# Recurrent states kept by pairs of heads instead of by threes in a fused mLSTM and mixture-of-experts kernel

## The chip, the cores and the metric

The kernel runs on one core of one Trainium2 chip. The metric is the device time of one execution, in microseconds (us). The core has a matrix engine (TensorE, PE in the profile), whose weight loads are listed as an engine of their own (PEld), a vector engine (DVE), a scalar engine (ACT), a general engine (POOL) and a queue engine that issues DMAs (SP). PE multiplies a stationary operand, which has to be loaded first, by a moving operand, and writes the products into banks of PSUM; a float32 multiplication is run as two passes over the same operands, and the trace lists each pass as a load and a matmul. So a group of three float32 matmuls stands there as x6.

## What is computed

An mLSTM layer (2 batches, 8 heads, 768 steps, heads of 40), then a dense feed-forward layer with 2048 hidden units, then 8 experts whose outputs are weighted by a gate that is normalised by rows and columns. Only the first part bears on the change:

```python
for t in range(S):
    m_new = np.maximum(f_gate[:, :, t] + m, i_gate[:, :, t])
    f_stab = np.exp(f_gate[:, :, t] + m - m_new)
    i_stab = np.exp(i_gate[:, :, t] - m_new)
    C = f_stab[..., None, None] * C + i_stab[..., None, None] * np.einsum('bhd,bhe->bhde', vt, kt)
    n = f_stab[..., None] * n + i_stab[..., None] * kt
    h_tilde = np.einsum('bhde,bhe->bhd', C, qt)
    nq = np.einsum('bhd,bhd->bh', n, qt)[:, :, None]
    y[:, :, t] = o * h_tilde / np.maximum(np.abs(nq), 1.0)
x = y.reshape(1536, 320)
x = np.maximum(0.01 * (x @ w_in), x @ w_in) @ w_out          # then the experts, on x
```

## The kernel before

The sequence is cut into 6 pieces of 128 steps, which with 2 batches makes 12 chunks (`c0` to `c11`; even ones belong to batch 0, odd ones to batch 1). Within a chunk the recurrence is a masked product: scores of keys and queries (`sc`), weighted by decays (`ap`, `ex`, `wg`), times the values (`va`). What crosses from chunk to chunk is a state per head, 40 keys by 41 columns (40 values and the normaliser). Three steps of a chunk deal with it:

- `state` (`dp`, line 619): the weighted keys `kw` of three heads side by side, 120 columns, are the stationary operand, and the values of the three heads, 123 columns, the moving one. Of the 3 by 3 blocks of the product only the diagonal ones are wanted. Eight heads make G = 3 groups, with a ninth head of zeros. Chunks 0 to 9 do it.
- `carry` (`cr`, lines 660 to 665): the product `dps` is multiplied by a table `bdm` that is 1 on the diagonal blocks, and added to the state `Cst`, which is multiplied by its decay `decC` in the same instruction: one DVE instruction of 120x369 and three of 120x123. In chunks 0 and 1 it is one instruction that writes the masked product.
- `recall` (`zp`, line 613): the queries of three heads, stacked on 120 rows, are the stationary operand (128 columns, one for each step), and `Cst` of the group is the moving one (123 columns). Chunks 2 to 11 do it. These queries come in a load of their own, `q3`; the scores use another copy, `qP`, in which head pairs lie on rows 0 to 39 and 64 to 103.

The decays of the states are made twice (`nL` and `qL`, line 475): three matmuls with a table `ex` of 120 columns, loaded by DMA, spread a decay of each head over the head's rows, and an exponential on ACT writes `decC`.

The first 41 steps of the dense layer (`u`: up, `d`: down) and chunks 0 to 5 are laid out by the table `ORDER`: each engine runs its instructions in the order of that table. On PE it also holds matmuls on zeros that nothing reads (`w8@p` is eight of them), which stand where PE would be idle. SP issues the loads in the table's order as well. From chunk 6 on the program is written by a loop, and a scheduler orders it. After the dense layer come the experts, which the change doesn't touch. A step of the dense layer is 8 matmuls up (line 223) and 12 down (lines 230 to 232); the down matmuls stand three steps behind the up ones in the loop.

At the start PE waits for the gates: SP loads gates and the small table `rco`; DVE runs scans over the gates (lines 412 to 431); ACT splits numbers in halves (`a5` and `a6`, lines 437 and 438); DVE joins them (`a7`, line 441, writes `mv`) and spreads them (`c0.bd`, line 559), which the first decay matmul of chunk 0 reads (`c0.ap0`, line 566). The output of chunk 0 (`c0.ou`, DVE line 643) is turned by PE (`c0.tt`, line 335). DVE weighs the keys of some chunks (`kw`, line 602), POOL those of others (`c1`, `c2`, `c3`); the masking of decays (line 576) and some low halves of weights (`px`, line 215) are POOL's too.

## Time and profile before

| | before |
|---|---|
| median of 3 runs | 931.91 us (931.9 to 932.8) |
| the profiled execution | 931.88 us |
| its span, first to last instruction | 930.1 us |
| PE busy | 924.2 us, 99% |
| DVE / ACT / POOL busy | 587.3 / 490.1 / 552.1 us |
| DMA engines, mean share of the first 25 us | 0.85 |

The 1.8 us between the profiled time and its span lie before the first and after the last instruction. Busy time of PE counts overlapping passes once, so it tells that PE has work, not that the work is dense; the views that show waits and the distances between passes are needed beside it.

### The profile page before, as it was taken

How to read it: one execution, taken by the hardware profiler on the slowest of the kernel's cores; microseconds unless marked ns; L12 is line 12 of the kernel's file. 1: busy time of each engine (PE TensorE's matmuls, PEld its weight loads, DVE VectorE, ACT ScalarE, POOL GpSimd, SP SyncE). 2: the span in 40 equal slices, each digit the busy share in tenths (PEclk: the TensorE clock that was granted, in tenths of full speed). 3: DMA queues.
4: the chain of work that ended last, by engine and by line, in shares of the span. 5: the costliest groups of instructions: out<-in, count | busy, mean ns of one | idle time of the engine just before them, and what ended most of it. 6: DMA issues, size and time to landing. Idle time of an engine off the chain costs nothing.

```text
span 930.1 us, 16892 instructions
## 1 busy us (share of the span) xinstructions
PE 924.2 (99%) x6192; PEld 903.2 (97%) x6192; DVE 587.3 (63%) x1180; ACT 490.1 (53%) x959; POOL 552.1 (59%) x574
## 2 busy tenths in 40 slices
PE   9999999999999999999999999999999999999998
PEld 5899999999999999999999999999999999999998
DVE  8998751523958587666656665665666565666655
ACT  6877445345763645555445445544544455454442
POOL 3330244443442756767777777777777777767762
PEclk9999999999999999999999999999999999999999
DMA  8773131110301110111111111111111111111002
GB/s 273 253 233 129 34 111 31 56 39 3 88 14 33 52 38 24 52 38 38 37 38 53 46 52 38 37 38 38 50 48 50 41 38 38 38 49 49 30 2 85
DMA packets 57384, 56.49 MB, mean 61 GB/s; under 512 B 7654, under 2 KB 48086, under 8 KB 57302
## 3 DMA queue, kind: packets, MB, share of 16 engines
q1 hardware_dynamic: 57302, 55.43, 19.7%
q8 instruction: 48, 0.79, 0.4%
q14 instruction: 34, 0.28, 0.1%
HBM read 53.43 MB, written 1.97 MB: 60 GB/s over the span
## 4 chain that ended last, share of the span: by engine, by line
PE 94%; DVE 3%; ACT 1%; DMA 1%; issue 1%; SPq 0%; ACTq 0%; DVEq 0%
PE y L230 12%; PE y L231 12%; PE y L232 12%; PE ha L223 9%; PE b L1030 8%; PE b L1031 8%; PE b L1033 8%; PE b L1032 8%; PE ya L230 3%; PE ya L232 3%; PE ya L231 3%; PE yps L607 2%; PE sps L591 1%; PE zps L613 1%; PE dps L619 1%
## 5 line engine op out<-in xcount | busy, mean ns | idle before, releaser
L1054 POOL TENSOR_TENSOR hl<-c,hh 128x384 fp32r<-128x384 f32 x192 | 197.3, 1028 | 180.2 <-ACT c L1053 155.5
L230 PE MATMUL y<-w_e,hh 128*128 128x320 f32 x768 | 238.6, 311 | 0.0
L231 PE MATMUL y<-w_e,hh 128*128 128x320 f32 x768 | 237.0, 309 | 0.0
L232 PE MATMUL y<-w_e,hl 128*128 128x320 f32 x768 | 236.9, 308 | 0.0
L1112 DVE SCALAR_TENSOR_TENSOR acc<-y,Pg,acc 128x320 f32<-128x320 f32 x336 | 179.1, 548 | 63.4 <-PE y L232 56.3
L1052 ACT ACTIVATE hh<-c 128x384 fp32r<-128x384 f32 x192 | 99.8, 520 | 208.5 <-DVE c L1049 208.5
L1030 PE MATMUL b<-X,w_e 128*128 128x384 f32 x448 | 152.7, 341 | 0.2 <-DVE s L1070 0.2
L1031 PE MATMUL b<-X,w_e 128*128 128x384 f32 x448 | 151.0, 337 | 0.0
L1033 PE MATMUL b<-X,w_e 96*128 96x384 f32 x448 | 151.0, 337 | 0.0
L1032 PE MATMUL b<-X,w_e 128*128 128x384 f32 x448 | 150.9, 337 | 0.0
L230 PEld LDWEIGHTS y<-w_e,hh 128*128 128x128 f32 x768 | 144.3, 188 | 1.7 <-DVE acc L1110 1.1
L231 PEld LDWEIGHTS y<-w_e,hh 128*128 128x128 f32 x768 | 144.3, 188 | 0.0
L232 PEld LDWEIGHTS y<-w_e,hl 128*128 128x128 f32 x768 | 144.2, 188 | 0.0
L1053 ACT ACTIVATE c<-c 128x384 f32<-128x384 f32 x192 | 101.0, 526 | 18.0 <-ACT hh L1052 0.7
L1049 DVE TENSOR_TENSOR c<-b,s 128x384 f32<-128x384 f32 x192 | 100.6, 550 | 13.4 <-PE b L1033 10.0
L223 PE MATMUL ha<-xT,w_a 128*128 128x256 f32 x768 | 107.8, 285 | 0.0
L223 PEld LDWEIGHTS ha<-xT,w_a 128*128 128x128 f32 x768 | 100.1, 190 | 1.1 <-ACT gg L712 0.2
L1077 DVE SCALAR_TENSOR_TENSOR hl<-b,hh 128x384 fp32r<-128x384 f32 x64 | 35.6, 557 | 95.4 <-ACT hh L1076 95.4
L723 POOL TENSOR_TENSOR hla<-gg,hha 128x256 fp32r<-128x256 f32 x64 | 49.3, 772 | 70.3 <-ACT hha L718 62.4
L259 POOL TENSOR_TENSOR raw_e<-raw_e 128x256 f32<-128x256 f32 x116 | 85.2, 743 | 4.5
L1030 PEld LDWEIGHTS b<-X,w_e 128*128 128x128 f32 x448 | 84.8, 189 | 1.3 <-DVE s L1070 0.6
L1031 PEld LDWEIGHTS b<-X,w_e 128*128 128x128 f32 x448 | 85.3, 190 | 0.0
(200 smaller groups left out, 1496.7 us busy)
## 6 DMA issues: line engine op xcount, KB each, us to landing
raw_e<-in_w_dram SPq DMA_DIRECT2D x31, 320.0 KB, 2.9
raw_e<-in_w_dram SPq DMA_DIRECT2D x62, 128.0 KB, 2.2
raw_e<-in_w_dram SPq DMA_DIRECT2D x248, 32.0 KB, 1.9
raws<-in_w_in_dram SPq DMA_DIRECT2D x8, 768.0 KB, 5.9
rawU<-in_w_out_dram SPq DMA_DIRECT2D x4, 640.0 KB, 5.6
R<-in_kp_dram SPq DMA_DIRECT2D x10, 256.0 KB, 3.4
R<-in_qp_dram SPq DMA_DIRECT2D x10, 256.0 KB, 3.6
raws<-in_w_out_dram SPq DMA_DIRECT2D x4, 640.0 KB, 4.6
```

The lines of the kernel that those rows point to most:

```text
L223: nc.tensor.matmul(h_ps, t1[:, ws, c * P:(c + 1) * P], xt[:, xs, t0:t0 + n], start=(j == 0), stop=(j == len(MM1) - 1),)
L230: nc.tensor.matmul(y_ps, a, t2[:, c, :], start=first, stop=False)
L231: nc.tensor.matmul(y_ps, a, t2[:, 2 + c, :], start=False, stop=False)
L232: nc.tensor.matmul(y_ps, b, t2[:, c, :], start=False, stop=last)
L1030: nc.tensor.matmul(bank, f[:, 0], b[:, 0], start=fresh, stop=False, skip_group_check=not fresh)
L1031: nc.tensor.matmul(bank, f[:, 0], b[:, 2], start=False, stop=False, skip_group_check=not fresh)
L1032: nc.tensor.matmul(bank, f[:, 2], b[:, 0], start=False, stop=False, skip_group_check=not fresh)
L1033: nc.tensor.matmul(bank, f[0:K3, 1], b[0:K3, 1], start=False, stop=True, skip_group_check=not fresh)
L1049: nc.vector.tensor_tensor(c, part, plus, op=ALU.add)
L1053: nc.scalar.activation(c, c, AF.Relu)
L1054: nc.gpsimd.tensor_tensor(hl[a][b], c, hh[a][b].bitcast(F32), op=ALU.subtract)
L1112: nc.vector.scalar_tensor_tensor(out=o, in0=y, scalar=Pg[:, 2 * HP * q + t, e:e + 1], in1=o, op0=ALU.mult, op1=ALU.add)
```

## The change

Heads are kept in pairs: G = 4 groups of two heads, on rows 0 to 39 and 64 to 103, as `qP` already has them.

- `recall` reads `qP` (rows 0 to 103); the load `q3` and its place are gone. `qP` of odd and even chunks has a place each, since it is now read later.
- `state` has 4 matmuls with 104 stationary columns (the weighted keys lie 64 apart, with zeros between) and 82 moving ones. `recall` has 4 with 128 and 82, the decays of the states 4 with 128 and 4 or 6.
- `carry` takes just the two diagonal blocks: two DVE instructions of 40 rows by 4x41, which copy (chunks 0 and 1) or add `dps` to the state. The rest of `Cst` stays zero from a memset at the start, so the table `bdm` goes, and with it half of the load `cst`.
- The decay of the state is a step of its own, `fade` (`cm`): one POOL instruction of 104x328, in chunks 2 to 9, after the recall.
- The ninth head goes from `vn` and `kw`. `kp` and `qp` are loaded on 104 rows. The table `ex` is made on ACT instead of being loaded.
- POOL's memsets at the start change: those of `lastG`, of part of `ex` and of the ninth head go, those of all of `kw` and of both `Cst` come.

```diff
-    G = 3
-    GW = 3 * D
-    GV = 3 * DV
+    G = 4
+    GO = 64
+    GW = GO + D
+    GV = 2 * DV
+    HALVES = ((slice(0, D), slice(0, DV)), (slice(GO, GW), slice(DV, GV)))
...
-    ident = cst[:, 0:P]
-    bdm = cst[:, P:P + GV]
+    ident = const.tile([P, P], F32, tag="cst", name="cst")
...
             for g in range(G):
-                nc.tensor.matmul(dpc[0:GW, g * B * n:(g + 1) * B * n], ex[:, 3 * g:3 * g + 3, :].rearrange("p h d -> p (h d)"),
+                nc.tensor.matmul(dpc[:, g * B * n:(g + 1) * B * n], ex[:, 2 * g:2 * g + 2].rearrange("p h d -> p (h d)"),
                                  lastG[:, :, c0:c1], start=True, stop=True)
...
             def load_qP(self):
-                self.qP = self.place([P, 4, P], "qP", "w2v")
-                nc.sync.dma_start(self.qP, qp[self.b, self.c])
+                self.qP = places[f"qP{self.ck % 2}"]
+                nc.sync.dma_start(self.qP[0:GW], qp[self.b, self.c, 0:GW])
...
-            def load_q3(self):
-                if self.c > 0:
-                    self.q3 = places["q3"][0:GW]
-                    nc.sync.dma_start(self.q3, q3[self.b, self.c])
...
-                        nc.tensor.matmul(self.zps[:, g * GV:(g + 1) * GV], self.q3[:, g, :], Csts[self.b][0:GW, g, :], start=True, stop=True)
+                        nc.tensor.matmul(self.zps[:, g * GV:(g + 1) * GV], self.qP[0:GW, g, :], Csts[self.b][0:GW, g, :], start=True, stop=True)
...
-                        nc.tensor.matmul(self.dps[0:GW, g * GV:(g + 1) * GV], kw[:, 3 * g:3 * g + 3, :].rearrange("p h d -> p (h d)"),
-                                         self.v[:, 3 * g:3 * g + 3, :].rearrange("p h d -> p (h d)"), start=True, stop=True)
+                        nc.tensor.matmul(self.dps[0:GW, g * GV:(g + 1) * GV], kw[:, 2 * g:2 * g + 2].rearrange("p h d -> p (h d)")[:, 0:GW],
+                                         self.v[:, 2 * g:2 * g + 2].rearrange("p h d -> p (h d)"), start=True, stop=True)
...
+            def fade(self, eng):
+                b, c, Cst = self.b, self.c, Csts[self.b]
+                if 0 < c < NCH - 1:
+                    eng.tensor_tensor(Cst[0:GW], Cst[0:GW], decC[0:GW, b, :, c:c + 1].to_broadcast([GW, G, GV]), op=ALU.mult)
+
             def carry(self):
-                    dm = places["dm"]
-                    nc.vector.tensor_tensor(dm[0:GW], dsrc, msk, op=ALU.mult)
-                    for g in range(G):
-                        nc.vector.scalar_tensor_tensor(out=Cst[0:GW, g, :], in0=Cst[0:GW, g, :], scalar=decC[0:GW, b, g, c:c + 1],
-                                                       in1=dm[0:GW, g, :], op0=ALU.mult, op1=ALU.add)
+                dsrc = self.dps[:, 0:G * GV].rearrange("p (g f) -> p g f", g=G)
+                for r, f in HALVES:
+                    state = Csts[self.b][r, :, f]
+                    if self.c == 0:
+                        nc.vector.tensor_copy(state, dsrc[r, :, f])
+                    else:
+                        nc.vector.tensor_tensor(state, dsrc[r, :, f], state, op=ALU.add)
...
-                 "ex": lambda: nc.sync.dma_start(sc0[0:R, 2 * S + 512:], scr_in[:, 512:]),
+                 "ex": lambda: nc.scalar.activation(ex, oh.unsqueeze(2).to_broadcast([R, 8, GO]), AF.Relu, scale=rc[:, 2:3]),
```

Of the table `ORDER`, `ex` moves forward from behind `f2` to behind `a9`, the loads `q3` go, and a step `cm` stands behind the `zp` (and ahead of the `kw`) of chunks 2 to 5. Three places show the moves. The first is PE from the state product of chunk 1 to the recall of chunk 2, before and then after; `dps` is the state product, `aps` a decay matmul, `dpc` the decays of the states, `zps` the recall, `pt_a` the turned output.

```order
L619 MATMUL dps_379<-vt_odd,R_76 120x123 x3
L566 MATMUL aps_2_388<-bd,stt_99 128x512
L568 LDWEIGHTS identb
L568 MATMUL aps_2_388<-mask,identb 128x512
L475 MATMUL dpc_392<-lastG,sc_95 120x6 x3
L613 MATMUL zps_401<-Cst_106,R_76 128x123 x3
L566 MATMUL aps_3_409<-bd,stt_100 128x512
L568 LDWEIGHTS identb
L568 MATMUL aps_3_409<-mask,identb 128x512
L335 MATMUL pt_a_419<-cst,R_76 128x128 x2
```

The same stretch of PE after:

```order
L615 MATMUL dps_380<-vt_odd,R_76 104x82 x4
L562 MATMUL aps_2_390<-bd,stt_99 128x512
L564 LDWEIGHTS identb
L564 MATMUL aps_2_390<-mask,identb 128x512
L477 MATMUL dpc_395<-lastG,sc_95 128x6 x4
L609 MATMUL zps_405<-Cst_106,R_76 128x82 x4
L562 MATMUL aps_3_415<-bd,stt_100 128x512
L564 LDWEIGHTS identb
L564 MATMUL aps_3_415<-mask,identb 128x512
L336 MATMUL pt_a_424<-cst,R_76 128x128 x2
```

The order is the same; three groups of three have become groups of four, with other widths.

The second is POOL from the spreading of chunk 2 (`bd`) to the masking of chunk 4, before and then after; lines 602 and 598 weigh the keys of chunks 1, 2 and 3, lines 215 and 216 are low halves of weights, line 653 is the fade.

```order
L559 TENSOR_TENSOR bd<-mv,rco 64x1024 x2
L602 TENSOR_TENSOR R_76<-kn_odd,Dm_odd 128x320
L215 TENSOR_TENSOR w_a_372<-raws_177,w_a_372 128x768
L602 TENSOR_TENSOR R_76<-R_76 128x320
L215 TENSOR_TENSOR w_a_415<-raws_197,w_a_415 128x768
L602 TENSOR_TENSOR R_76<-kn_odd,Dm_odd 128x320
L215 TENSOR_TENSOR w_a_555<-raws_177,w_a_555 128x768
L215 TENSOR_TENSOR w_a_644<-rawU,w_a_644 128x640
L576 AFFINE_SELECT R_76<-R_76 128x1024
```

The same stretch of POOL after:

```order
L555 TENSOR_TENSOR bd<-mv,rco 64x1024 x2
L598 TENSOR_TENSOR R_76<-kn_odd,Dm_odd 128x8x40
L216 TENSOR_TENSOR w_a_373<-raws_178,w_a_373 128x768
L653 TENSOR_TENSOR Cst_106<-Cst_106,decC 104x328
L598 TENSOR_TENSOR R_76<-R_76 128x8x40
L216 TENSOR_TENSOR w_a_420<-raws_196,w_a_420 128x768
L598 TENSOR_TENSOR R_76<-kn_odd,Dm_odd 128x8x40
L653 TENSOR_TENSOR Cst_107<-Cst_107,decC 104x328
L216 TENSOR_TENSOR w_a_560<-raws_178,w_a_560 128x768
L653 TENSOR_TENSOR Cst_106<-Cst_106,decC 104x328
L216 TENSOR_TENSOR w_a_648<-rawU,w_a_648 128x640
L572 AFFINE_SELECT R_76<-R_76 128x1024
```

The fade of chunk 2 now stands ahead of the weighing of that chunk's keys, the fade of chunk 3 behind that of chunk 3, and the fade of chunk 4 ahead of a low half and of the masking.

The third is ACT at the start, before and then after; lines 437 and 438 (439 and 440) are the halves of `a6` and then of `a5`, and `mv` is what `a7` reads.

```order
L437 ACT_TABLE_LOAD
L437 ACTIVATE sc_96<-sc_95,rco 64x128
L438 ACTIVATE sc_95<-sc_95 64x128
L850 ACTIVATE identb<-cst 128x128
L437 ACTIVATE sc_95<-sc_96,rco 64x128
L438 ACTIVATE mv<-sc_96 64x128
L437 ACTIVATE sc_96<-sc_95,rco 64x256
```

The start of ACT after:

```order
L439 ACT_TABLE_LOAD
L439 ACTIVATE sc_96<-sc_95,rco 64x128
L440 ACTIVATE sc_95<-sc_95 64x128
L846 ACTIVATE identb<-cst 128x128
L847 ACTIVATE sc_95<-rco 64x512
L439 ACTIVATE sc_95<-sc_96,rco 64x128
L440 ACTIVATE mv<-sc_96 64x128
L439 ACTIVATE sc_96<-sc_95,rco 64x256
```

The making of `ex`, 64x512, stands between the halves of `a6` and those of `a5`.

## Rows read from the trace of the kernel before

**Rows 1.** The page: busy time of the engines, PE's granted clock in slices.

```profile
PE 924.2 (99%) x6192; PEld 903.2 (97%) x6192; DVE 587.3 (63%) x1180; ACT 490.1 (53%) x959; POOL 552.1 (59%) x574
...
PEclk9999999999999999999999999999999999999999
```

**Rows 2.** Waits of PE: who waited for whom, total us, times, longest.

```profile
PE warm L901 <- DVE R L834: 1.4, 1, 1.4
PE dps L456 <- issue: 0.4, 1, 0.4
PE pt_a L335 <- DVE R L643: 0.2, 1, 0.2
PE b L1030 <- DVE s L1070: 0.2, 1, 0.2
```

**Rows 3.** Chain of waits, 0 to 60 us: start us, us, what.

```profile
24.36 0.50 DVE R L643
...
25.63 1.71 PE yps L607 x16
...
27.99 0.64 PE dps L619 x6
...
38.64 0.67 PE zps L613 x6
```

**Rows 4.** PE's timeline, two windows: start us, us, instructions merged [idle before].

```profile
9.20 1.89 PE L882 MATMUL warm<-R 128*128 128x512 bf16 x8
11.21 0.50 PE L566 MATMUL aps<-bd,stt 96*128 96x512 f32 x1
...
20.20 0.79 PE L475 MATMUL dpc<-lastG,sc 96*120 96x4 f32 x6
...
21.86 2.97 PE L882 MATMUL w<-R 128*128 128x512 bf16 x13
25.00 0.41 PE L335 MATMUL pt_a<-cst,R 128*128 128x128 f32 x2 [0.17 <-DVE R L643]
...
29.48 0.91 PE L613 MATMUL zps<-Cst,R 120*128 120x123 f32 x6
...
30.47 0.39 PE L568 MATMUL aps<-mask,identb 128*128 128x512 bf16 x1
30.91 0.41 PE L335 MATMUL pt_a<-cst,R 128*128 128x128 f32 x2
...
32.79 0.80 PE L619 MATMUL dps<-R 128*120 128x123 f32 x6
```

**Rows 5.** Weight loads by form: xcount | busy us, mean ns | idle before.

```profile
L613 PEld LDWEIGHTS zps<-Cst,R 120*128 120x128 f32 x60 | 7.6, 191 | 0.2 <-ACT R L573 0.2
L619 PEld LDWEIGHTS dps<-R 128*120 128x120 f32 x48 | 5.9, 183 | 0.0
```

**Rows 6.** ACT's timeline, the second half of `a5`.

```profile
8.20 0.29 ACT L438 ACTIVATE mv<-sc 64x128 fp32r<-64x128 f32 x1
```

**Rows 7.** DVE's timeline ahead of and at the join `a7`.

```profile
8.50 0.41 DVE L428 TENSOR_TENSOR sc<-sc 64x256 f32<-64x256 f32 x1
8.83 0.33 DVE L441 SCALAR_TENSOR_TENSOR mv<-mv,rco,sc 64x128 f32<-64x128 f32 x1
```

**Rows 8.** ACT by line and form, 0 to 60 us: 512 columns.

```profile
L573 ACT ACTIVATE R<-aps 128x512 f32<-128x512 f32 x6 | 3.5, 588 | 1.2 <-PE aps L568 1.2
```

**Rows 9.** POOL's timeline: the weighing of the keys of chunks 2 and 3.

```profile
29.86 0.98 POOL L602 TENSOR_TENSOR R<-R 128x320 f32<-128x320 f32 x1 [0.20 <-ACT R L573]
...
36.11 0.74 POOL L602 TENSOR_TENSOR R<-kn_odd,Dm_odd 128x320 f32<-128x320 f32 x1 [2.58 <-ACT ha L712]
```

**Rows 10.** DVE by form, 0 to 230 us: the carries, and a small one.

```profile
L665 DVE SCALAR_TENSOR_TENSOR Cst<-Cst,decC,R 120x123 f32<-120x123 f32 x24 | 9.2, 413 | 0.1
...
L663 DVE TENSOR_TENSOR R<-dps,cst 120x369 f32<-120x369 f32 x8 | 4.2, 530 | 0.0
...
L635 DVE TENSOR_TENSOR den<-R,den 128x8 f32<-128x8 f32 x10 | 2.2, 219 | 0.2
```

More of the change, by code (lines that the diff above doesn't have):

```diff
@@ L30 @@
 ORDER = """
-m0 gA gN gF rco a0 cst a1 a2 L3 n0 c0.kP a3 n1 a4 c0.kn n2 c0.qP f0 a6 L1 c0.v n4 im a9 a5 L0 a8 f1 n3 c1.kP n6 a7 nT@0
-c1.qP f2 ex c0.bd og0 pl3 L2 pu3 c2.q3 f4 w8@p c0.ap0@1 n8 c1.v c1.ap1@2 n5 f3 c1.kn w1@p c1.ap0@3 n9 c0.ex0 pa3
-c0.ap1@1 n7 c0.sc c0.ex1 pb3 c1.ex0 c2.bd qT@1 c1.ex1 c0.wg pu1 pl1 w8@p c0.va@3 nS c0.kw ph3 pa1 qTe pl0 px3 c0.dp@2
-pb1 pu0 c1.sc c0.cr nTe ph1 pa0 nL@1 px1 c2.ap1@0 nLe sg0 pb0 c3.ap1@2 L5 c2.kP c4.bd c0.dn c2.qP c1.wg c2.v c2.kn L7
-pu2 c0.sg c3.kP c0.ou c2.ex1 c1.kw w13@h c0.tt@1 pl2 c1.va@3 qS pa2 c0.xi ph0 pb2 w3@h c1.dp@0 c3.ex1 px0 c0.xl pl5
@@ L46 @@
-d15 g17 pl14 h17 u18 pu14 l17 c5.sg pa12 u19 g18 h18 pl13 d16 pb12 g19 l18 d17 h19 l19 u20 pa14 u21 pa13 g20 ph12 pb13
-d18 h20 g21 l20 d19 h21 pb14 ph15 u22 l21 e19 u23 g22 h22 ph13 d20 l22 wl px12 g23 d21 h23 ph14 l23 u24 px14 d22 g24 h24
-u25 l24 px15 u26 g25 px13 d23 c5.ou g26 h25 h26 d24 l25 l26 f9 c5.tt@3 u27 c4.tt@1 g27 u28 h27 l27 f7 d25 g28 c5.cr
-c4.xi u29 d26 c4.xl g29 h28 h29 d27 l28 l29 u30 e27 u31 g30 c5.xi h30 d28 ws c5.xl c6.bd g31 h31 l30 l31 c4.cr
+m0 gA gN gF rco a0 cst a1 a2 L3 n0 c0.kP a3 n1 a4 c0.kn n2 c0.qP f0 a6 L1 c0.v n4 im a9 ex a5 L0 a8 f1 n3 c1.kP n6 a7
@@ L57, in mlstm_moe_kernel @@
     nc = tc.nc
-    B, NCH, P = qp.shape[0:3]
+    B, NCH = qp.shape[0:2]
+    P = 128
     S = NCH * P
@@ L88, in mlstm_moe_kernel @@
     R3 = R + 32
-    cst = const.tile([P, P + GV], F32, tag="cst", name="cst")
+    ident = const.tile([P, P], F32, tag="cst", name="cst")
     rco = const.tile([R, 14], F32, tag="rco", name="rco")
-    ident = cst[:, 0:P]
-    bdm = cst[:, P:P + GV]
     oh = rco[:, 0:8]
@@ L479, in last_exp @@
             c0, c1 = a // P, z // P
-            nc.scalar.activation(decC[0:GW, :, :, c0:c1],
-                                 decay_banks[a, z][0:GW, 0:G * B * (c1 - c0)].rearrange("p (g b c) -> p b g c", g=G, b=B), AF.Exp)
+            nc.scalar.activation(decC[:, :, :, c0:c1],
+                                 decay_banks[a, z][:, 0:G * B * (c1 - c0)].rearrange("p (g b c) -> p b g c", g=G, b=B), AF.Exp)
         decay_banks = {}
@@ L552, in load_rest @@
                 self.load_v()
-                self.load_q3()
                 self.load_kn()
@@ L645, in attend_all @@
             def attend_all(self):
+                self.fade(nc.gpsimd)
                 self.recall_scale()
@@ L840, in mlstm_moe_kernel @@
         nc.gpsimd.affine_select(out=causal, in_=causal, pattern=[[1, P]], compare_op=ALU.is_ge, fill=NEG, base=0, channel_multiplier=-1)
-        nc.gpsimd.memset(kw[:, 8, :], 0.0)
-        for t in (stt[0].bitcast(F32), stt[1].bitcast(F32), bd[R:R3].bitcast(F32), lastG, G3[R:R3], ex[R:R3], own):
+        for t in (stt[0].bitcast(F32), stt[1].bitcast(F32), bd[R:R3].bitcast(F32), G3[R:R3], own, kw, Csts[0], Csts[1]):
             nc.gpsimd.memset(t, 0.0)
@@ L864, in chunk_tasks @@
             n = f"c{c.ck}."
-            for k in ("kP", "qP", "v", "q3", "kn"):
+            for k in ("kP", "qP", "v", "kn"):
                 tasks[n + k] = getattr(c, f"load_{k}")
@@ L870, in chunk_tasks @@
             tasks[n + "sg"] = lambda: c.gate(engine(n + "sg"))
+            tasks[n + "cm"] = lambda: c.fade(nc.gpsimd)
             if c.ck % 2 == 0:
```

62 lines of the change are left out of this document (32 added, 30 removed).

## The prediction, made before the changed kernel was run

> **What bounds the kernel now.** First the page: PE is busy 99% of the span at full granted clock, every other engine at most 63% [rows 1]. Busy time alone could hide loose work, so next the waits of PE: four in all, together 2.2 us, and the one of 1.4 us is the wait for the first memset [rows 2]. The chain of waits says the same by time: up to 25.0 us it runs through loads, ACT and DVE, and from the turn of chunk 0's output on it is PE, pass behind pass [rows 3]. So the kernel has two parts. In the first 25 us DVE's order of work decides, and PE fills its time with matmuls on zeros. Behind that the time is the sum of PE's passes. A pass added there is paid in full, and a DVE instruction or a load saved there is worth nothing, unless somebody makes PE wait.
>
> What does a pass of a small float32 matmul cost? The chain has groups of them [rows 3]: the values, 128 stationary columns and 41 moving ones, 1.71 us for 16 passes, 107 ns each; the state product, 120 and 123, 0.64 us for 6, 107 ns; the recall, 128 and 123, 0.67 us for 6, 112 ns. The decays of the states move only 4 columns, and 6 passes span 0.79 us [rows 4]; less some 0.25 us for the last one's own length that is (0.79 - 0.25) / 5 = 108 ns. From 4 to 123 moving columns the price is the same. So the pass is as long as its weight load, and fewer moving columns don't shorten it. The load itself depends on the stationary columns: 191 ns long for 128, 183 for 120, 8 ns for 8 columns [rows 5].
>
> **What the change adds on PE.** Three groups become four, so 6 passes become 8, at these prices:
> - Recall, chunks 2 to 11: 128 stationary columns as before, 8 x 0.112 = 0.896 us for 0.67, +0.226 each, +2.26 in ten.
> - State product, chunks 0 to 9: 104 stationary columns for 120. No row has a load of 104. At the least it costs 16 x 1 ns less than the 120 (91 ns, by the two loads above), at the most the same 107. In proportion it is 107 x 104 / 120 = 93 ns; I take that, since it lies near what the loads show: 8 x 0.093 = 0.744 for 0.64, +0.10 each, +1.0 in ten. Ends: +0.9 and +2.2.
> - Decays of the states, twice: 8 x 0.112 = 0.896 for 6 x 0.107 = 0.64, +0.26 each, +0.52.
>
> Together +3.78 us of PE work.
>
> The Trainium skill ("TensorE: Matmul & The Clock Gate", LDWEIGHTS) gives a load as the stationary columns by 1.2 GHz, whatever the number of rows: 87, 100 and 107 ns for 104, 120 and 128 columns. By it the sum would be 0.93 + 2.13 + 0.51 = 3.6 us, an estimate from that page; the loads here agree in kind [rows 3, 5].
>
> **What of it is absorbed.** PE stands still a little where the order makes it wait for DVE. At 25.0 us it waits for chunk 0's output: 13 unread passes from 21.86, of 216 ns by (2.97 - 0.38) / 12, end at 24.67, so 0.33 us are free [rows 4]. At 30.91 the turn of chunk 1's output comes 0.44 us behind the masking matmul at 30.47, where such a matmul takes 0.23, so 0.21 are free [rows 4].
>
> **What it moves at the start.** ACT now makes `ex`, 512 columns, between the halves of `a6` and of `a5`. An activation of 512 columns lasts 0.59 us [rows 8]; since one starts before the one ahead has drained, I take 0.5 for its place in the row. The second half of `a5` ended at 8.49 [rows 6], and DVE, busy with line 428 until then, joined at 8.83 [rows 7], so 0.3 of the 0.5 are hidden, and the join, the spread behind it and PE's first decay matmul come 0.2 us later. PE was waiting there already: 8 unread passes from 9.20 end at 10.92, the matmul starts at 11.21 [rows 4]. If ACT's step were hidden wholly, that is 0; if DVE had no slack, 0.5.
>
> The carry of chunk 0 on DVE was one instruction of about 0.54 us and is two copies of 164 columns on 40 rows; each costs between a tiny one's 0.22 and the 0.53 of 369 columns [rows 10]. In the middle 0.33 each: +0.1 us ahead of chunk 0's output (ends -0.1 and +0.5). So the output comes 0.3 us later, and the turn at 25.3. PE arrives at 24.67 + 0.2 + 0.10 (state of chunk 0) + 0.26 (decays) = 25.23. The start costs 0.3 us.
>
> **The sum.** Start 0.30; behind it PE 3.78 - 0.36 = 3.42; less 0.21 at chunk 1's turn, where DVE moves by 0.5 and PE by 0.9: 0.30 + 3.42 - 0.21 = 3.5 us. The profiled execution took 931.88 us and the median is 931.91, the same for this purpose. 931.9 + 3.5 = **935.4 us**.
>
> **What I cost at nothing.** From chunk 2 on a carry on DVE falls from one instruction of 0.53 and three of 0.41 to two: some 8 x 1.1 = 9 us less DVE work. PE hides it: behind 31 us no wait of PE for DVE is longer than 0.2 [rows 2]. If that cover were gone, the gain would show. Ten loads `q3`, the table's load and the smaller loads of `kp`, `qp`, `vn` and `cst` relieve SP and the DMA engines; the chain has no load in it after `rco`, and so nothing waits for them. `qP` is read until the recall now, but odd and even chunks have a place each, so a load waits for the recall two chunks back. POOL's memsets change before anyone reads what they fill. The eight fades cost POOL 0.7 to 1.0 us each by the instruction of 320 columns [rows 9]; in the loop a low half behind a fade has three steps of slack before PE reads it.
>
> **Rivals.** (a) *Narrow loads are no cheaper.* The state product pays 107 ns a pass: +1.1 to +1.2 us, 936.5. For it: the chain's 107 ns for both 120 and 128 columns. Against: the two load lengths.
>
> (b) *The fade becomes a wait of PE.* In chunk 2 POOL must fade before it weighs the keys (it is in order), and the fade waits for the recall to end, at 29.48 + 0.91 = 30.39 before [rows 4], 31.3 then (0.3 of start, 0.10, 0.26 and 0.23). With 0.74 to 0.98 us for each of the two [rows 9] the keys are ready at 32.8 to 33.3; PE reads them at 32.79 [rows 4] plus 0.7, 33.5, its weights 0.2 earlier. So it comes out even, and 0.1 to 0.5 us are lost if POOL is slower than the 320 columns show, as with a decay that is spread along the row: 935.9. Fade and masking in chunk 4 have about the same slack. DVE would wait too, with the carry in its row and chunk 2's output behind it.
>
> (c) *Not slower: moving columns decide.* If a pass cost by what it moves, 82 for 123 columns, 8 recall passes would take 8 x 0.112 x 82 / 123 = 0.60 us for 0.67 and the state product 0.57 for 0.64: -1.4 us in twenty groups, the decays unchanged, +0.3 of start and +0.5: 931.3, no change that can be told. It decides from the point where the moving operand takes longer than the load. Against it stand the 41 columns of the values at 107 ns and the 4 of the decays at 108. The Trainium skill (same page, Back-to-back issue gap) has such a rule for a single stream, moving columns by 2.4 GHz plus 2.5 ns; by it these passes would be short, and the rows here disagree, since each has a weight load of its own.
>
> (d) *DVE's relief reaches PE at the start* (both copies cheap, ACT's step hidden, and PE's small waits further on filled too): 0.3 less at the start, 0.5 less behind it, and 8 recall passes at 107 ns, 0.4 less: 934.2. Still slower.
>
> **Chances.** Forecast with its small errors 0.64, (a) 0.10, (b) 0.11, (c) 0.08, (d) 0.05, something unseen that makes it faster 0.02. A measurement of this kernel tells some 0.2%, 1.9 us, from no change. Slower by more than that begins at 933.8. Forecast, (a), (b) and three fifths of (d), which lies close to that line, make slower 0.88; (c) and the rest of (d) make same 0.10; faster is 0.02. The range runs from just below (d) to (a) with (b)'s half microsecond: 934.0 to 936.9, and leaves out (c), the unseen and the worst of (a) and (b) together.
>
> **What would show it.** After: recall groups of 8 passes at 0.112 us and state groups of 8 at about 0.093, in the chain; PE busy about 3.5 us more; the passes of lines 609, 615 and 477 at 80, 80 and 16; the join `a7` at about 9.0 and the turn of chunk 0 at about 25.3; no new wait of PE above 0.3 us; the chain still PE from there on. Wrong would be: state passes at 107 ns (a), a wait of PE for POOL's keys or for a carry (b), recall passes near 75 ns (c). If PE's work grows as reckoned and the time doesn't, PE waited before where these views show none.

## The result and the profile after

| | before | after |
|---|---|---|
| median | 932.05 us (931.85 to 932.87, 8 runs) | 936.47 us (935.9 to 942.49, 8 runs) |
| the profiled execution | 931.88 us | 935.9 us |
| its span | 930.1 us | 934.2 us |

The changed kernel is slower by half a per cent: ratio 1.0055, 95% interval 1.0045 to 1.0066. The median lies in the predicted range (934.0 to 936.9); the ratio, which is above that of the medians (1.0047), times the 931.91 us of the prediction gives 937.0, just above the range. The eight executions after are 935.9, 936.03, 936.15, 936.3, 936.65, 937.32, 939.2 and 942.49; the two longest had a mean granted clock of 0.998 and 0.994, the others 1.0. So two things have to be explained: some 4 us in every execution, and a tail of 1 to 6 us in some, which the kernel before doesn't have. I call executions above 937 us long, the others common. The five common ones have a mean of 936.2, all eight 937.5.

First the page of the changed kernel, as in [rows 1]: busy time by engine, and PE's granted clock by slices.

```profile
PE 926.9 (99%) x6233; PEld 906.8 (97%) x6236; DVE 586.0 (63%) x1166; ACT 490.9 (53%) x960; POOL 558.4 (60%) x582
...
PEclk9999999999999999999999999999999999999999
```

PE is busy 2.7 us more (3.5 were forecast; PE's idle time before 10 us is 1.0 longer), and still 99% of its span. POOL has 6.3 us more from the fades. DVE has 1.3 us less. Summed by steps, its carries of chunks 2 to 9 fell from 14.1 us to 5.2, the 9 us of the prediction; but some of its other steps, unchanged in number and size, grew: nine low halves (`w_a`) from 9.0 to 10.9 us, twenty of the experts' steps on `rawx` from 10.1 to 12.3. The two that grew most start within 0.7 us of a fade on POOL: a low half at 52.77 us with 3.47 for 1.90, and a step on `rawx` at 128.81 with 1.78 for 0.42. That steps of DVE grow beside POOL's returns below. The waits of PE, as in [rows 2]: who waited for whom, total us, times, longest.

```profile
PE dps L458 <- issue: 1.5, 1, 1.5
PE warm L898 <- DVE R L831: 1.3, 1, 1.3
PE aps L562 <- DVE bd L555: 0.4, 1, 0.4
PE pt_a L336 <- DVE R L639: 0.3, 1, 0.3
PE dps L615 <- POOL R L598: 0.2, 1, 0.2
```

The first two lie before 10 us, and the first one's size differs from run to run (0.41 in the repeated kernel): the granted clock rose to 1.0 at 5.50 us here and at 7.04 in the trace of before, so that the twenty unread passes took 6.57 us for 7.27. New since [rows 2] are 0.4 at the first decay matmul (the prediction allowed no new wait above 0.3), 0.1 more at the turn of chunk 0's output, and 0.2 for POOL's keys in chunk 2. Of that last wait some 0.1 is real: the unread pass ahead of it has its weight load in the trace, at 34.18 us, but no record of its own. The chain of the changed kernel between 40 and 56 us, as in [rows 3]: start us, us, what.

```profile
45.44 0.71 PE dps L615 x8
...
51.16 0.85 PE zps L609 x8
```

A state product is 0.71 us for 0.64, a recall 0.85 for 0.67, both still PE's own time. Last PE's timeline, as in [rows 4]: start us, us, instructions merged, [idle before].

```profile
20.79 0.95 PE L477 MATMUL dpc<-lastG,sc 64*128 64x4 f32 x8
...
22.92 2.75 PE L879 MATMUL w<-R 128*128 128x512 bf16 x12
25.98 0.41 PE L336 MATMUL pt_a<-cst,R 128*128 128x128 f32 x2 [0.32 <-DVE R L639]
...
32.56 0.38 PE L336 MATMUL pt_a<-cst,R 128*128 128x128 f32 x2
```

The turn of chunk 0 has moved from 25.00 [rows 4] to 25.98, that of chunk 1 from 30.91 to 32.56. The span ends 4.1 later. So 1.0 is lost by the first mark, 1.65 by the second, and 2.4 behind it.

### The profile page after: what moved, and what is told of

Read it like the earlier page. It is cut to its first block, busy times and chain, and to the rows that moved or that the text cites. A ratio compares the mean times of both kernels' runs of the same rounds, so it can differ in the third digit from the quotient of the medians.

```text
span 934.2 us, 16956 instructions
## 1 busy us (share of the span) xinstructions
PE 926.9 (99%) x6233; PEld 906.8 (97%) x6236; DVE 586.0 (63%) x1166; ACT 490.9 (53%) x960; POOL 558.4 (60%) x582
## 3 DMA queue, kind: packets, MB, share of 16 engines
HBM read 50.00 MB, written 1.97 MB: 56 GB/s over the span
## 4 chain that ended last, share of the span: by engine, by line
PE 96%; ACT 1%; SPq 1%; DVE 1%; issue 1%; POOL 0%; DMA 0%; POOLq 0%; DVEq 0%; ACTq 0%
PE y L231 12%; PE y L232 12%; PE y L233 12%; PE ha L224 10%; PE b L1027 8%; PE b L1028 8%; PE b L1030 8%; PE b L1029 8%; PE ya L231 3%; PE ya L233 3%; PE ya L232 3%; PE yps L603 2%; PE sps L587 1%; PE zps L609 1%; PE dps L615 1%; PE aps L562 1%
```

## Experiments

All are compared with the kernel before on the same chip, and with the changed kernel, which was run again beside e13, e14 and e16 alone; elsewhere that comparison is between chips. Times in us, those of a row in order of size:

| kernel | executions | median | ratio to before, 95% |
|---|---|---|---|
| before (four groups of runs) | 931.3 to 933.5, 51 runs | 931.8 to 932.3 | |
| after, again | 935.72, 935.97, 935.97, 936.89, 939.12 | 935.97 | 1.0037 to 1.0062 |
| e9 before, a fourth group | 936.24, 936.33, 936.33, 936.37, 936.49 | 936.33 | 1.0031 to 1.0057 |
| e10 after, state of 128 columns | 937.34, 937.54, 938.24, 938.38, 940.14 | 938.24 | 1.0043 to 1.0071 |
| e1 `ex` back | 936.05, 936.11, 936.13, 936.5, 938.29 | 936.13 | 1.0037 to 1.0064 |
| e3 more zeros | 935.75, 935.76, 936.15, 936.45, 937.42 | 936.15 | 1.0033 to 1.0059 |
| e4 before, fewer zeros | 932.19 to 932.54 (3), 933.6 to 934.1 (8) | 933.76 | 1.0006 to 1.0024 |
| e5 `ex` loaded | 935.71, 936.02, 936.05, 936.2, 940.42, 940.91 | 936.12 | 1.0038 to 1.0076 |
| e8 before, with the fade | 932.17 to 932.7 (9), 934.78, 936.83 | 932.39 | 1.0000 to 1.0020 |
| e16 before, fourth group and fade | 936.11, 936.55, 936.72, 936.78, 939.61 | 936.72 | 1.0041 to 1.0067 |
| e2 keys first | 937.1, 937.72, 939.19, 939.28, 940.48 | 939.19 | 1.0060 to 1.0085 |
| e6 keys first, sign step later | 936.3, 936.41, 936.44, 936.5, 937.15 | 936.44 | 1.0035 to 1.0059 |
| e7 sign step later | 936.92, 937.24, 938.5, 939.48, 940.27 | 938.5 | 1.0050 to 1.0077 |
| e13 sign step behind the carry | 935.43, 935.48, 935.52, 935.68, 935.88 | 935.52 | 1.0024 to 1.0051 |
| e14 e13, `ex` loaded, more zeros | 935.39, 935.56, 935.94, 935.96, 936.87 | 935.94 | 1.0028 to 1.0054 |
| e11 fade on DVE | 938.27, 938.28, 938.45, 938.78, 941.3 | 938.45 | 1.0056 to 1.0082 |
| e12 before, gate early | 934.21, 934.55, 934.81, 936.79, 937.3, 937.35 | 935.8 | 1.0023 to 1.0048 |

### The passes

The theory is the prediction's: what counts is the weight load, and two more passes per group are paid. The rival is that moving columns decide and the loss has another source. The first kernel adds passes to the kernel before, and nothing else (the products of the fourth group aren't read):

```diff
-                    for g in range(G):
+                    for j, g in enumerate((0, 1, 2, 2)):
-                        nc.tensor.matmul(self.zps[:, g * GV:(g + 1) * GV], self.q3[:, g, :], Csts[self.b][0:GW, g, :], start=True, stop=True)
+                        nc.tensor.matmul(self.zps[:, j * GV:(j + 1) * GV], self.q3[:, g, :], Csts[self.b][0:GW, g, :], start=True, stop=True)
...
```

> The kernel before, in threes, with a fourth group of passes, a repeat of the third, in recall, state product and decays of the states: only PE's work grows, and what the fourth pass computes is read by nobody. Theory (each pass is paid by its weight load): recall 10 x 0.22, state 10 x 2 x 0.107 = 10 x 0.21, decays 2 x 0.26, in sum 4.8, less 0.4 to 0.6 absorbed at 25 and 31 us: 936.1 to 936.5, with little spread. Rival (moving columns decide, and the changed kernel's loss comes from its start and its fades): under 933.

Measured 936.33, 4.5 more than the 931.78 of before beside it, all five within 0.25 us. The second widens the stationary operand of the changed kernel's state product:

```diff
-                        nc.tensor.matmul(self.dps[0:GW, g * GV:(g + 1) * GV], kw[:, 2 * g:2 * g + 2].rearrange("p h d -> p (h d)")[:, 0:GW],
+                        nc.tensor.matmul(self.dps[:, g * GV:(g + 1) * GV], kw[:, 2 * g:2 * g + 2].rearrange("p h d -> p (h d)"),
```

> The changed kernel with 128 stationary columns for 104 in the state product: the 24 more compute sums that nobody reads. Theory (a pass costs its weight load): the state's passes go from 92 to 112 ns, chunks 0 to 9 cost 10 x 8 x 0.02 = 1.6 us more, 937.7 to 938.0. Rival (a load of 104 columns is no cheaper, the other reading of the loads): passes alike, the time within 0.3 us.

Measured 938.24, a little above what was expected; all but one lie at 937.3 to 938.4. Two rows of e9's chain, a recall (128 stationary and 123 moving columns) and a state product (120 and 123):

```profile
40.26 0.89 PE zps L613 x8
...
45.21 0.85 PE dps L619 x8
```

And a state product in e10's chain, 128 stationary and 82 moving columns:

```profile
45.78 0.85 PE dps L615 x8
```

For 8 state passes the chain has 0.71 us with 104 stationary columns, 0.85 with 120 and 123 moving, 0.85 with 128 and 82 moving. The narrow load is cheaper. The moving columns don't show: two recall passes stand 112 ns apart with 123 moving columns in e9 and with 82 in the changed kernel. The median distance of two state passes is 92 ns in the changed kernel and 112 ns in e10. Both rivals (a) and (c) fall.

### The start

Four kernels deal with the first 26 us. In e1 ACT's making of `ex` goes back to where its load stood:

```diff
-... n4 im a9 ex a5 L0 a8 f1 n3 c1.kP n6 a7 nT@0 c1.qP f2 c0.bd ...
+... n4 im a9 a5 L0 a8 f1 n3 c1.kP n6 a7 nT@0 c1.qP f2 ex c0.bd ...
```

> The changed kernel with the making of the table ex on ACT moved back in the order, to where its load stood before (behind the first scan of the last gates), so that it no longer stands between the halves of a6 and a5. Theory (ex at the head of DVE's chain): the join a7, the first decay matmul and the turn of chunk 0's output come 0.3 to 0.6 us earlier than in the changed kernel's profile (turn at 25.4 to 25.7 for 25.98), and the time falls by as much, to about 936.0; fewer long runs, if the wait of PE ahead of the first decay matmul (0.59 us there) is what lets the clock fall. Rival (the start moved because rco landed 0.3 us later, or because of the copies of the state): the turn stays within 0.15 us of 25.98 and the time stays.

Measured 936.13. The join came at 9.03 (9.44 in the changed kernel, 8.83 before) and the first decay matmul at 11.40 (11.82), as expected. But the turn stood at 26.03. The 0.7 us of ACT now held up ACT's row later, and DVE's weighing of chunk 0 started at 15.39 behind a wait of 0.31. The step's time is paid wherever it stands, since ACT's row is on the way to the turn. In e5 the table is loaded instead, so that the step is gone:

```diff
-                 "ex": lambda: nc.scalar.activation(ex, oh.unsqueeze(2).to_broadcast([R, 8, GO]), AF.Relu, scale=rc[:, 2:3]),
+                 "ex": lambda: nc.sync.dma_start(sc0[0:R, 2 * S + 512:], scr_in[:, 512:]),
...
```

> The changed kernel with ex loaded with the constants (512 columns of 9 rows wider) in place of ACT's step. Theory (ACT's step costs the start up to 0.6 us of its row, and the copies of chunk 0's state the rest): ACT's row at 8 to 9 us is 0.6 shorter, the join a7 comes near 8.9 to 9.1 for 9.44, chunk 0's weighing is not held up by ACT (line 593 near 15.0), the turn of chunk 0 stands at 25.4 to 25.6 for 25.98, and the time is 0.3 to 0.5 us less than the changed kernel's common executions: 935.6 or so. Rival (the gates' loads, not ACT, set the start): the turn stays near 25.9 and the time at 936.1.

DVE's timeline in the kernel before, in the changed kernel and in e5 (lines 660 and 662 are the carry of chunk 0, and the line behind is the next step):

```profile
19.22 0.54 DVE L660 TENSOR_TENSOR Cst<-dps,cst 120x369 f32<-120x369 f32 x1
19.68 1.02 DVE L193 TENSOR_SCALAR raws<-raws 128x768 uint8<-128x768 uint8 x1
```

```profile
19.90 0.67 DVE L662 COPY Cst<-dps 40x164 f32<-40x164 f32 x2
20.59 1.02 DVE L194 TENSOR_SCALAR raws<-raws 128x768 uint8<-128x768 uint8 x1
```

```profile
19.60 0.67 DVE L662 COPY Cst<-dps 40x164 f32<-40x164 f32 x2
```

In e5 all of DVE's row is 0.30 earlier, and the turn stands at 25.68. The two copies take 0.69 us from their start to the next one's (19.90 to 20.59), where the one instruction of before took 0.46 (19.22 to 19.68): +0.23. But the time is 936.12, no less than with ACT's step. The two profiled executions keep 0.30 of distance up to 127 us, where 0.25 of it goes. There the first weight load of a recall in e5 waits for an exponent on ACT (line 569), which the changed kernel's load doesn't:

```profile
127.18 0.97 PEld L609 LDWEIGHTS zps<-Cst,R 104*128 104x128 f32 x8 [0.17 <-ACT R L569]
```

And ACT's row ahead of that exponent starts with a step that waits for a load of output gates, at the same time in the changed kernel and in e5:

```profile
121.31 1.28 ACT L407 ACT_TABLE_LOAD   x1 [2.85 <-DMA R<-in_og_dram]
```

```profile
121.31 1.28 ACT L407 ACT_TABLE_LOAD   x1 [3.17 <-DMA R<-in_og_dram]
```

So what the start gains can be lost again at a load 100 us on. The last two kernels change the number of unread passes at the very start, e3 in the changed kernel, e4 in the kernel before:

```diff
-            for _ in range(20):
+            for _ in range(27):
```

> The changed kernel with 27 for 20 unread passes at the very start, which fill the 1.5 us in which PE stood idle ahead of the turn of the first decays. Theory (the long runs come from a clock that falls back after this idle time): no execution with a mean granted clock under 0.9995, all runs within 1 us, median 936.0. Rival (the spread comes from the steady part, from POOL's fades or from DMA): executions of 937 to 942 remain, one in three.

```diff
-            for _ in range(20):
+            for _ in range(14):
```

> The kernel before with 14 for 20 unread passes at the very start, so that PE stands idle there as long as or longer than in the changed kernel. Theory (idle time at the start lets the clock fall in some executions): some executions of 934 to 940 with a mean granted clock under 0.9995, where the kernel before has none above 932.9. Rival (the spread belongs to the changed kernel's own work): all runs between 931.8 and 933.

In e3 the idle time ahead of line 458 was gone, and nothing else moved by more than `rco` did (936.15, one execution at 937.42, all at a full clock). In e4 eight of eleven executions took 933.6 to 934.1 us, seven of them at a granted clock of 0.996 to 0.998. So idle time at the start can cost 1.5 us in some executions. It isn't the only source of the tail, since e3, which has none, still has a long execution; and e9 and e13, whose profiled executions have 1.36 and 1.43 us of it, have no long one in five each. That it adds to the tail isn't excluded.

### The long executions

The first hint came from an attempt to take 0.2 us from PE by weighing chunk 2's keys ahead of the fade:

```diff
-... c2.zp@0 c2.cm pu5 c1.sg L4 c2.kw c3.ap0@2 ...
+... c2.zp@0 pu5 c1.sg L4 c2.kw c2.cm c3.ap0@2 ...
```

> The changed kernel with the fade of chunk 2 moved behind the weighing of that chunk's keys on POOL. Theory (the fade ahead of the keys makes PE wait 0.38 us at 34.4): the wait goes, the state product of chunk 2 follows the unread pass at once, 0.3 to 0.4 us less, unless the carry of chunk 2 on DVE then waits for the fade. Rival (the keys waited for something else): no change at 34.4.

It missed: all five are long, three with a clock of 0.998, and one of these was profiled. To see why, look at two engines in the same few microseconds. In the kernel before, DVE's `pa5` (line 193, a sign step on 640 columns of bytes) starts just ahead of a low half on POOL (line 215). DVE's row, then POOL's:

```profile
31.09 0.88 DVE L193 TENSOR_SCALAR raws<-raws 128x640 uint8<-128x640 uint8 x1
```

```profile
31.36 2.17 POOL L215 TENSOR_TENSOR w_a<-raws,w_a 128x768 fp32r<-128x768 f32 x1 [0.52 <-ACT w_a L211]
```

The same steps in the changed kernel, where line 653 is the fade and 598 the keys:

```profile
32.68 1.21 DVE L194 TENSOR_SCALAR raws<-raws 128x640 uint8<-128x640 uint8 x1
33.92 0.29 DVE L345 TENSOR_TENSOR xT<-pt_a,xT 64x128 fp32r<-64x128 f32 x1
```

```profile
32.31 0.74 POOL L653 TENSOR_TENSOR Cst<-Cst,decC 104x328 f32<-104x328 f32 x1 [1.92 <-PE zps L609]
33.01 1.38 POOL L598 TENSOR_TENSOR R<-R 128x320 f32<-128x320 f32 x1
34.34 1.88 POOL L216 TENSOR_TENSOR w_a<-raws,w_a 128x768 fp32r<-128x768 f32 x1
```

And in e2, with PE behind them and, last, the granted clock (the stretch, its length, busy time of PE, PEld, DVE, ACT and POOL, and then the clock, third from the end):

```profile
32.96 2.72 DVE L194 TENSOR_SCALAR raws<-raws 128x640 uint8<-128x640 uint8 x1
...
36.02 0.42 DVE L346 TENSOR_TENSOR xT<-pt_a,xT 128x256 fp32r<-128x256 f32 x1
```

```profile
32.37 0.74 POOL L653 TENSOR_TENSOR Cst<-Cst,decC 104x328 f32<-104x328 f32 x1 [0.61 <-PE zps L609]
33.07 1.85 POOL L216 TENSOR_TENSOR w_a<-raws,w_a 128x768 fp32r<-128x768 f32 x1
```

```profile
36.50 1.10 PE L224 MATMUL ha<-xT,w_a 128*128 128x256 f32 x7 [0.81 <-DVE xT L346]
```

```profile
39.10:42.50 3.40, 3.40 (x16) 3.21 (x16) 2.71 (x8) 0.86 (x3) 0.00 (x0) 0.50 0.61 182
```

The durations tell who waited. Alone the byte step takes 0.88 us, the keys 0.74, the low half 1.86. Before, DVE was first, and POOL's 2.17 holds 0.3 of waiting. After, the fade was first: DVE's 1.21 holds 0.33, until the fade ends at 33.05, and then POOL's keys (1.38) waited for DVE. In e2 DVE again arrived during the fade, but POOL's next step got in ahead of it, and DVE's 2.72 holds the whole low half. What follows is in PE's row: the low halves of chunk 1's turned output (line 346) come at 36.02 for 34.22, PE stands still for 0.81 us, and from 39.10 to 42.50 its granted clock is 0.50, that is 1.2 GHz for 2.4.

The Trainium skill ("SBUF — State Buffer", Who interferes with whom) says that DVE and POOL share one pair of ports, and that of two instructions that need it the one that issues first holds it for its whole length while the other blocks. The durations here agree (0.88 to 2.72 for the same step, the excess ending with POOL's instruction). Which of the two goes next when one waits and the other has a further step ready, the runs show both ways.

If that is the cause, moving `pa5`, the byte step, helps. A first way, behind chunk 1's turned output, with the keys first (e6) and without (e7):

```diff
-... c1.tt@1 pa5 c3.kn c2.sc@30 c1.xi px2 c3.ex0 c1.xl f6 ...
+... c1.tt@1 c3.kn c2.sc@30 c1.xi px2 c3.ex0 c1.xl pa5 f6 ...
```

> The kernel with keys ahead of the fade in chunk 2, and DVE's sign step pa5 moved from ahead of chunk 1's second transpose result (c1.xl) to just behind it. Theory (POOL's fade and low half, back to back, stretch pa5 from 0.9 to 2.7 us on DVE; chunk 1's output comes late, PE waits 0.8 us at its first up matmul, and the granted clock falls to a half for 3.4 us): with pa5 behind, DVE L345 and L346 come near 33.9, no wait of PE above 0.3 us near 36.5, all executions at a granted clock of 1.0, 935.7 to 936.3. Rival (something else stretches DVE there): executions of 939 to 940 remain in about half the cases, as with the keys first and the sign step in its old place.

> The changed kernel with one step moved: DVE's sign step pa5 behind chunk 1's second transpose result (c1.xl). Theory (the long executions come from POOL's fade and what follows it, which stretch pa5 on DVE and with it chunk 1's output): no execution over 937 us, all at a granted clock of 1.0, common ones at 936.0 to 936.3 (the passes stay). Rival (they come from the idle time at the start): one or two in five at 937 to 942 still.

e6 came nearly as expected: all five at a clock of 1.0, where e2 had 937.1 to 940.5, but at 936.3 to 937.15 for the expected 935.7 to 936.3, so that one of them still counts as long. e7 didn't: all five between 936.92 and 940.27. DVE's, POOL's and PE's rows in e7:

```profile
34.30 1.97 DVE L194 TENSOR_SCALAR raws<-raws 128x640 uint8<-128x640 uint8 x1
36.04 1.33 DVE L593 TENSOR_TENSOR R<-sps,R 128x512 f32<-128x512 f32 x2
```

```profile
33.62 1.86 POOL L216 TENSOR_TENSOR w_a<-raws,w_a 128x768 fp32r<-128x768 f32 x1
```

```profile
36.83 0.41 PE L603 MATMUL yps<-R 128*128 128x41 f32 x2 [0.63 <-DVE R L593]
```

The step had been moved from the fade onto the low half. Chunk 2's weighing (line 593) now stood behind it, and PE waited for that instead. In e6 the keys were done earlier, the low half ended at 34.55, and the same step took 1.09. So the step must stand where PE waits for nothing behind it: behind chunk 2's carry.

```diff
-... c1.tt@1 pa5 c3.kn ... c2.cr pu4 c2.va@1 ...
+... c1.tt@1 c3.kn ... c2.cr pa5 pu4 c2.va@1 ...
```

> The changed kernel with DVE's sign step pa5 behind chunk 2's carry (c2.cr), so that it stands neither ahead of chunk 1's turned output nor ahead of chunk 2's weighing. Theory (POOL's fade shifts POOL's low half onto a DVE step that PE waits behind; which of the two yields differs between executions): POOL's row at 32 to 36 us meets only DVE steps that give PE its time, DVE L345 comes near 33.7 and L593 near 34.3, no wait of PE over 0.3 us at 36 to 37, fewer or no executions over 937 us, common ones at 936.0 to 936.4. Rival (the long executions come from another place): as many over 937 as in the changed kernel beside it.

> The changed kernel as it is, on the same chip as the others. Common executions at 935.9 to 936.5, and one or two in five over 937 with a granted clock below 1.0.

DVE's row in e13, then POOL's:

```profile
34.16 1.28 DVE L593 TENSOR_TENSOR R<-sps,R 128x512 f32<-128x512 f32 x2
...
36.04 0.89 DVE L194 TENSOR_SCALAR raws<-raws 128x640 uint8<-128x640 uint8 x1
```

```profile
33.48 1.86 POOL L216 TENSOR_TENSOR w_a<-raws,w_a 128x768 fp32r<-128x768 f32 x1
```

The byte step and the low half take what they take alone, PE waits for nobody there, the five executions lie within 0.45 us (below the expected 936.0 to 936.4), and the median is 0.45 under that of the changed kernel on the same chip, which had one long execution in five. The intervals of the two ratios overlap; but of the 29 executions of the changed kernel, e1, e3 and e5, which all have `pa5` in its place, 8 are long, and none of the 10 of e13 and e14. If each were long with a chance of 8 in 29, ten without one would have a chance of 0.04; for eight long ones spread at random over all 39 it is 0.07. So this points to `pa5` and doesn't prove it. e14 joins e13, the loaded `ex` and the 27 unread passes:

> The same with ex loaded in place of ACT's step and 27 unread passes at the start for 20. Theory: the turn of chunk 0 at 25.4 to 25.7, no executions over 937, common ones at 935.5 to 936.0: what is left over before is the price of the passes, some 3.5 us. Rival: what the start gains is lost further on, 936.1.

It gives 935.94, no better than e13. Its turn stands at 25.60, e13's at 25.76, and PE's last matmul ends at 930.58 and 930.54; the lead is lost at the same recall near 127 us.

Two kernels put the fade into the kernel before, alone (e8) and with the fourth group (e16):

```diff
+                    eng.tensor_tensor(Cst[0:GW], Cst[0:GW], decC[0:GW, b, :, c:c + 1].to_broadcast([GW, G, GV]), op=ALU.mult)
...
-                        nc.vector.scalar_tensor_tensor(out=Cst[0:GW, g, :], in0=Cst[0:GW, g, :], scalar=decC[0:GW, b, g, c:c + 1],
+                        nc.vector.scalar_tensor_tensor(out=Cst[0:GW, g, :], in0=Cst[0:GW, g, :], scalar=1.0,
```

> The kernel before, in threes, with one part of the change alone: the decay of the states of inner chunks is a step of POOL of 369 columns in the places where the changed kernel has its fades, and DVE's carry multiplies by 1. PE's passes are those of before. Theory (the passes make the +3.5 us, the fade makes the spread): common executions at 932.0 to 932.5, and in some of them the granted clock falls below 1.0 and the time is 934 to 940. Rival 1 (the fade costs every execution, by PE's waits for the keys): all at 932.6 or more. Rival 2 (the fade costs nothing, the long executions have another cause): all within 931.6 to 932.9, as before.

> The kernel before, in threes, with both parts: a fourth group of passes that repeats the third (recall, state, decays), and the decay of the states as POOL's fade, DVE's carry multiplying by 1. Theory (the two add up): 936.3 of the passes and 0.3 of the fade, 936.5 to 936.9 in the common executions, and one in five above 938. Rival (they are one thing, each needs the other's place): 936.3, without long executions.

The fade alone costs 0.6 us in the median (the interval begins at 1.0000) and brings a tail into a kernel that has none: 934.78 at a clock of 0.998 and 936.83 at 0.996, of eleven. With the fourth group the common ones rise to 936.1 to 936.8, and one of five is long. Passes and fade, without the changed kernel's start and carry, make about its time, and its tail; e16's state passes are the dearer ones of 120 columns.

Where the 0.6 us come from, e8's profile, a common execution, shows in part, and it isn't at `pa5`. In chunk 4 a small DVE step (line 634, 0.16 us in the kernel before) meets POOL's masking. DVE's, POOL's and PE's rows in e8:

```profile
53.37 1.05 DVE L634 TENSOR_SCALAR den<-R 128x8 f32<-128x8 f32 x1
```

```profile
52.58 1.81 POOL L576 TENSOR_SCALAR_AFFINE_SELECT R<-R 128x1024 f32<-128x1024 f32 x1
```

```profile
55.20 0.41 PE L232 MATMUL ya<-w_a,hla 128*128 128x320 f32 x1 [0.42 <-DVE hla L729]
```

The changed kernel has a collision at the same place, the low half of 3.47 us at 52.77, in e13 too, but no wait of PE behind it in either profile. Which of the two places makes the two high times of e8 isn't shown.

A collision needs no fade, though. In e10, which was to widen a load, the profiled execution shows another: DVE makes a low half itself (line 216) while POOL makes one. DVE's, POOL's and PE's rows, and the granted clock:

```profile
69.13 2.34 DVE L216 TENSOR_TENSOR w_a<-raws,w_a 128x768 fp32r<-128x768 f32 x1
```

```profile
68.93 1.73 POOL L216 TENSOR_TENSOR w_a<-rawU,w_a 128x640 fp32r<-128x640 f32 x1 [0.24 <-ACT w_a L212]
```

```profile
72.13 0.42 PE L603 MATMUL yps<-R 128*128 128x41 f32 x2 [0.28 <-DVE R L593]
```

```profile
74.60:78.00 3.40, 3.40 (x18) 3.40 (x17) 2.85 (x4) 1.32 (x3) 0.15 (x1) 0.50 0.47 185
```

In the changed kernel the same DVE step started at 67.81, ahead of POOL's at 68.45, and took 0.95. What moves one of the two rows against the other by half a microsecond can turn the order round.

### Two misses

e11 has the fade of chunks 2 to 5 on DVE:

```diff
-            tasks[n + "cm"] = lambda: c.fade(nc.gpsimd)
+            tasks[n + "cm"] = lambda: c.fade(nc.vector)
```

> The changed kernel with the fades of chunks 2 to 5 on DVE for POOL, at the same places of the order. Theory (POOL's fade next to other POOL work is what stretches DVE's sign step): pa5 lasts 0.9 us for 1.2, the fade itself costs DVE some 0.5, so chunk 1's low halves come near 34.1 as in the changed kernel; no execution over 937 us, common ones at 936.0 to 936.5. Rival (the fade's amount of work, not its engine, makes the long executions): they remain.

It tells nothing on the tail: at its place the fade makes DVE wait 1.23 us for the recall, ahead of chunk 1's output; PE waits 1.1 for that, and four of the five executions take 938.3 to 938.8. The byte step took 1.60 us there, not the expected 0.9. e12 was a try at a kernel that beats the one before, with chunk 0's output earlier:

```diff
-... c2.ap1@0 nLe sg0 pb0 c3.ap1@2 ... c0.ou c2.ex1 c1.kw w13@h ...
+... c2.ap1@0 sg0 c3.ap1@2 ... c0.ou pb0 nLe c2.ex1 c1.kw w9@h ...
```

> The kernel before with chunk 0's output earlier: ACT's sigmoid ahead of its exponent for the decays of the states, DVE's join pb0 behind chunk 0's output, and 9 unread passes for 13. If the turn of chunk 0 decides the start, it comes 0.6 to 0.9 us earlier (24.1 to 24.4 for 25.00), and the time is 0.5 to 0.9 less than before: 931.0 to 931.4. Rival (what was moved, pb0 and the exponent, is missed further on): 931.9 or more.

It is 3.5 us slower. DVE's row in e12, then ACT's and PE's:

```profile
23.13 1.25 DVE L640 TENSOR_TENSOR R<-R,den 128x320 f32<-128x320 f32 x1
...
27.44 2.53 DVE L199 SCALAR_TENSOR_TENSOR raws<-raws 128x768 int32<-128x768 int32 x1
```

```profile
24.96 0.19 ACT L480 ACTIVATE decC<-dpc 120x12 f32<-120x12 f32 x1
```

```profile
25.20 0.44 PE L335 MATMUL pt_a<-cst,R 128*128 128x128 f32 x2 [1.04 <-ACT decC L480]
...
30.88 0.76 PE L475 MATMUL dpc<-lastG,sc 96*120 96x6 f32 x6 [1.55 <-DVE xT L345]
```

The output step (0.49 before) met POOL's spreading of chunk 2, but chunk 0's output was ready at 24.90; PE's wait of 1.04 us ended with the exponent on ACT that the edit had moved back, at 25.15. So the edit itself ate this gain, as the rival in the expectation has it. Then a join (0.97 for the one ahead of it) met POOL's low half from 27.29 to 29.15, and PE waited 1.55 us behind it. From 32.75 to 39.58 its clock was at a half. So no version here beats the kernel before. e13 beats the changed kernel, but what it mends the kernel before doesn't have.

## Why the prediction was wrong, and where it was right

**The passes: right.** From the first pass of a group to the next other matmul, summed over all groups of the two traces, the recall takes 8.83 us for 6.71 (+2.12; forecast +2.26), the state product 7.08 for 5.92 (+1.16; forecast +1.0), the decays 1.86 for 1.21 (+0.66; forecast +0.52). Together +3.94 for +3.78. The choice of 93 ns for a load of 104 columns, between 91 and 107, was good (92); e9 and e10 show that it is the load that is paid.

**What is absorbed: about right.** From the first mark to PE's last matmul the trace has 3.3 us more (4.26 less 0.98), where the passes behind 26 us add 3.94 - 0.06 - 0.23 = 3.65. So 0.4 is absorbed there for a forecast of 0.21; the distance of the two traces wanders by 0.2 us in the experts, which the change doesn't touch, so it can't be told finer.

**The start: mis-sized.** Forecast +0.30 at the turn of chunk 0; measured +0.98 in the profiled execution, +0.68 in the one of the repeated kernel, +0.76 in e13. Four parts make the 0.98. The load `rco` landed 0.3 later (ACT's row begins at 5.88 for 5.58), which is chance: +0.2 in e1, +0.1 in e3, nothing in the repeated kernel, whose +0.68 is the start's cost without it. ACT's step takes 0.61 of ACT's row for 0.5, and e5, where `rco` landed as late, shows 0.30 of it at the turn, for 0.2. The copies cost +0.23 for +0.1: the nearest row, that of 369 columns with 0.53, would have given +0.5, the tiny one -0.1, and I took the middle. And DVE waited 0.1 for PE's state product ahead of them. What the start is worth in time the runs don't settle: e5 and e14 bring the turn 0.3 and 0.2 forward and are no faster; in their profiles the lead is lost near 127 us. The turn also slips without the change's start: in e9 it stands at 26.01, and DVE's output step there took 1.05 us beside POOL's keys.

**What I cost at nothing: here it failed.** The step that failed is the price of the eight fades on POOL, which the sum has at nothing and the range at 0.5 us at most. The prediction asked of the fade whether POOL's products would be late, and found "three steps of slack" for a low half behind a fade, and a tie in chunk 2, rival (b). The tie was right: PE lost some 0.1 us at the keys, where this group of state passes takes 0.75 us and most take 0.67 to 0.71, and in e2, with the keys ahead of the fade, the weight load of that group follows the unread pass's at once (34.49 behind 34.43). But POOL's step has a second victim, DVE, whose step beside it is stretched, and behind DVE stands PE. The prediction held DVE's row to be relieved, let DVE wait for the fade through the carry alone, and looked at no other step of it. In the traces of e7 and e2 this is a wait of PE of 0.63 and 0.81 us, and in e2 a stretch at half clock behind it; by them I explain the tail. Alone, the fade costs 0.6 us in the median and makes two high times of eleven (e8). Five of the eight long executions with `pa5` in its place have a clock below 1.0. A stretch of 3.4 us at a half lacks 1.7 us of full clock, 0.002 of the span; 942.49 with 0.994 lacks 5 us by that.

**The sum.** Common executions lie at 935.7 to 936.9 and e13 at 935.5, for a forecast of 935.4. The start would be 0.4 of that, if it is paid in full, and the passes 0.16. That e13 lies within 0.1 is luck in part: its turn is 0.5 later than forecast (25.76 for 25.3). By the common executions alone (936.2) the forecast's range would have held; what lifts the ratio over it is the tail, for which the range had no term. The sign and rival (b) as the place to look were right; of rival (b), the mechanism was wrong.

**What stays open.** No profile caught a long execution of the changed kernel itself, so that its tail comes from `pa5` and POOL is argued from e2, e6, e7 and e13 together, not shown by its own rows. The collision in chunk 4 and the idle time at the start (e4) may add to it.

## What to carry to other kernels

Small float32 matmuls in groups were paid here by the stationary columns of their loads, with 4 to 123 moving columns, so packing fewer heads into more groups cost time although each group moved less. When a step is given to an engine that seems half idle, ask not only when its product is needed, but whom it keeps from running beside it: here a kernel with one more POOL step of 0.74 us in each of eight chunks had a tail of 1 to 6 us on 8 of 29 executions. Behind the deciding engine's first wait, put the steps that may be stretched where nobody waits for what comes after them.
